# The decay tables of a retention and two-MLP kernel: loaded whole, or made on the chip from a few rows

## The chip, the core and the metric

The kernel runs on one core of one Trainium2 chip. The metric is device microseconds of one launch; the kernel before took 865.12 us, the median of three runs (864.43 to 865.42). The engines are named as in the profile: PE is TensorE, DVE is VectorE, ACT is ScalarE, POOL is GpSimd, SP is the engine that issues most loads. SPq and ACTq are the streams that issue DMAs; PEld is PE's weight load.

## What is computed

A retention layer (attention without softmax, with a decay in its place) is followed by two MLPs on the same 2304 tokens:

```
scores = scale * q @ k.T                      # 4 batches, 8 heads, 576 positions, head width 64
Dmat   = where(rel >= 0, gamma_h ** rel, 0)   # rel = position of query - position of key
x  = (scores * Dmat) @ v                      # as 2304 x 512
h  = x @ w_in;  y = max(0.01 * h, h) @ w_out  # 512 -> 2048 -> 512
h2 = y @ w2_in; out = where(h2 > 0, h2, exp(min(h2, 0)) - 1) @ w2_out
```

## The kernel before

**Tiling.** The 576 positions are cut into four chunks of 128 (`CH`) and a tail of 64, and each chunk is worked on for the four batches in turn: step `s` is chunk `s // 4`, batch `s % 4`. For a step of the first chunk (s = 0 to 3) `att_a(s)` makes the scores of 8 heads with 8 f32 products of 64x128 by 128 columns, and DVE multiplies them by the table `first` (gamma to the power of the distance, masked, times scale), into two tiles `pm`; `att_x(s)` multiplies with v; ACT rounds the sum to `xh` and DVE makes the rest `xl`. Later chunks use a running state `st`: their scores are multiplied by the table `later_sb` (line 222 and 226), and their result by the table `ot_sb` (line 281). `att_kv` updates the state; `att_w` on POOL multiplies the keys or values by decays from `sm_sb`.

**The MLPs.** Weights are loaded as 128 rows at a time and split into two parts of reduced precision: `split_a` (two ACT operations, `u` and `last`), `split_b` (four DVE operations, lines 356 to 363), `split_c` (ACT `wih` or `woh`, then `wil` or `wol` on POOL for the first four weights of each kind). `moe_h` and `moe_y` are the products of a unit of work; `moe_y` runs three units (`LAG`) behind `moe_h`, so the first three units have no `moe_y`.

**Order.** Nothing is reordered: each engine runs its instructions as they are written. The part that the change touches is the start, lines 596 to 656. Loads are issued by SP in the order written. Eight semaphores are dealt out to the loads of all queues in turn, and a load waits until the one that had its semaphore before has landed; so at most eight are in flight. `wake(n)` issues n bf16 products of 512 columns whose result nobody reads. The start is: nine wakes, `att_a(0)`, nine wakes, the split of the first weight, `att_a(1)`, `att_x(0)`, and so on to `att_kv(0)`; then come the units n = 0, 1, 2, ..., each with one `moe_h` and, while there are any, one attention step.

**Buffers.** The tag "pm" has four buffers: two for each `pm` pair and the `kn` tiles. The tag "raw" has three: `first` has one, the raw weights the others. The PSUM tags "y" and "h" have four banks each.

Of the kernel before, what the change touches and what calls it, by code (L numbers as in the profile page):

```python
# [9 lines left out]
F32 = mybir.dt.float32  # L10
# [3 lines left out]
AF = mybir.ActivationFunctionType  # L14
ALU = mybir.AluOpType

B, H, S, D = 4, 8, 576, 64
NT, DM, DFF = B * S, H * D, 2048
P = 128
NPAIR = H // 2  # L20
CH = 128
HC = CH // 2
# [17 lines left out]
WARM = 9  # L40
# [5 lines left out]
def _turned(x):  # L46

    x = x.copy()
    x[:, ::2] = np.roll(x[:, ::2], HC, axis=0)
    return x  # L50


def _decays():

    gamma = (1.0 - 2.0 ** (-5.0 - np.arange(H, dtype=np.float32))).astype(np.float64)
    scale = 1.0 / np.sqrt(D)
    pos = np.arange(CH)
    mask = (pos[None, :] >= pos[:, None]).astype(np.float64)
    ot = scale * gamma[:, None] ** (pos + 1.0 - CH)
    ot = np.repeat(ot.reshape(NPAIR, 2, 1, CH), D, axis=2)  # L60
    ot = ot.transpose(1, 2, 0, 3).reshape(P, NPAIR, CH)
    vt = _turned((gamma[:, None] ** (CH - 1.0 - pos)).T[:, :, None])[:, :, 0]
    gt = np.repeat((gamma**CH).reshape(NPAIR, 2, 1), D, axis=2).transpose(1, 2, 0).reshape(P, NPAIR)
    small = np.concatenate([vt, gt], axis=1)
    rel = pos[None, :] - pos[:, None]
    first = scale * gamma[None, :, None] ** np.maximum(rel, 0)[:, None, :] * mask[:, None, :]
    first = _turned(first).reshape(CH, NPAIR, 2, CH).transpose(2, 0, 1, 3)
    later = gamma[None, :, None] ** (CH - 1.0 - pos)[:, None, None] * mask[:, None, :]
    later = _turned(later).reshape(CH, NPAIR, 2, CH).transpose(2, 0, 1, 3)

    near = np.concatenate([later[1, :HC], later[0, HC:]]).reshape(CH, -1)
    far = np.concatenate([later[0, :HC], later[1, HC:]])[:, :, HC:].reshape(CH, -1)
    first = first.transpose(1, 0, 2, 3).reshape(CH, -1)
    later = np.concatenate([near, far], axis=1)
    return (
        np.ascontiguousarray(first, dtype=np.float32),
        np.ascontiguousarray(later, dtype=np.float32),
        np.ascontiguousarray(ot, dtype=np.float32),
        np.ascontiguousarray(small, dtype=np.float32),
    )  # L80


@with_exitstack
def retention_moe(
# [6 lines left out]
    w1_out: bass.AP,  # L91
    w2_in: bass.AP,
    w2_out: bass.AP,
    first: bass.AP,
    later: bass.AP,
    otab: bass.AP,
    small: bass.AP,
    out: bass.AP,
):
    nc = tc.nc  # L100
    NMAX = max(SIZES)
# [7 lines left out]
    gpool = ctx.enter_context(tc.tile_pool(name="gpool", bufs=2))  # L109
# [3 lines left out]
    def bank(tag, bufs):  # L113
        return psum.tile([P, 512], F32, tag=tag, bufs=bufs, name=f"ps_{tag}")
# [10 lines left out]

    pf = [cpool.tile([P, NPAIR, HC], F32, name=f"pf{j}") for j in range(2)]
    half = [slice(0, D), slice(D, P)]

# [52 lines left out]
    pm = {}  # L181
# [413 lines left out]

    with tc.manual_schedule():
        qk, v, k = slice(0, 2), slice(2, 3), slice(3, 4)
        load_step(0, [qk])
        nc.scalar.dma_start(out=sm_sb, in_=small)
        nc.sync.dma_start(out=first_sb, in_=first.rearrange("p (j n) -> p j n", j=2))  # L600
        load_next()
        load_step(1, [qk])
        load_step(0, [v])
        load_step(2, [qk])
        load_step(1, [v])
        load_step(3, [qk])
        load_step(2, [v])
        load_step(3, [v])
        load_step(0, [k])
        load_next()  # L610
        load_step(1, [k])
        load_step(4, [0])
        load_step(2, [k])
        load_step(3, [k])
        nc.sync.dma_start(out=later_sb, in_=later)
        load_step(4, [1])
        load_near(4)
        load_step(4, [2])
        nc.sync.dma_start(out=ot_sb, in_=otab)
        for z in pf:  # L620
            nc.vector.memset(z, 0.0)
        idle = pf[0].bitcast(BF16).rearrange("p a n -> p (a n)")
        warm = bank("h", 4)

        def wake(n):
            for _ in range(n):
                nc.tensor.matmul(warm, idle[:, :P], idle, start=True, stop=True)  # L627

        def step0(s):
            out_of = att_x(s, "h", 4)  # L630
            att_w(s)
            return out_of

        wake(WARM)
        att_a(0, "y", 4)
        wake(WARM)
        key = splits.pop(0)
        split_a(key)
        split_b(key)
        att_a(1, "y", 4)  # L640
        step0(0)()
        split_c(key)
        att_a(2, "y", 4)
        step0(1)()
        att_a(3, "y", 4)
        step0(2)()
        step0(3)()
        into_state = att_kv(0, "y", 4)
        del ain[0]
        load_step(5)  # L650
        load_near(5)
        load_next()
        load_near(6)
        load_near(7)
        load_next()
        begun = [splits.pop(0)]
        split_a(begun[0])
        ld, nxt = B + 2, B

        def ends_block(n):  # L660

            p = units[n - LAG] if 0 <= n - LAG < len(units) else None
            return p is not None and p[3][-1] == FQ - 1 and p[:2] != (0, 0)

        def begin(n):
            if not ends_block(n + 1) and may_split(n):
                begun.append(splits.pop(0))
                split_a(begun[-1])

        for n in range(len(units) + LAG):  # L670
            u = units[n] if n < len(units) else None
            p = units[n - LAG] if n >= LAG else None
            s = nxt if nxt < nsteps else None
            rounded, begun = begun, []
            for key in rounded:
                split_b(key)
                load_next()
            if n > 0:
                begin(n)
            else:  # L680
                att_q(nxt)
                att_w(nxt)
            if u:
                moe_h(u)
            for key in rounded:
                split_c(key)
            if n == 0:
                into_state()
                att_a(nxt, "h", 4)
                for a in range(1, B):  # L690
# [78 lines left out]
```

## Time and profile before

| | before |
|---|---|
| median of 3 runs | 865.12 us (864.43 to 865.42) |
| the profiled execution | 864.54 us, of which its span is 862.6 us |
| PE busy | 851.8 us, 99% |
| DVE busy | 503.6 us, 58% |
| ACT busy | 346.8 us, 40% |
| POOL busy | 84.3 us, 10% |
| read from HBM | 54.66 MB |
| loads of tables | `first` 512 KB, `later_sb` 384 KB, `ot_sb` 256 KB, `sm_sb` 6 KB |

All times of the trace are microseconds from the start of the span. The profiled execution took 1.9 us more than its span, and is 0.58 us below the median of the three runs. Busy shares are means over the whole span; the stages of the first 52 us differ from the rest, and have to be read by themselves.

### The profile page before, as it was taken

The page shows a single profiled execution, that of the slowest core. Times are in us where ns is not written, and L with a number is a line of the kernel's source. Part 1 is how long each engine was busy: PE and PEld are TensorE (multiplying, and loading weights), DVE is VectorE, ACT ScalarE, POOL GpSimd, SP SyncE. Part 2 cuts the span into 40 slices and gives each one's busy share as a digit, 9 for nine tenths or more (in the row PEclk, how much of TensorE's full clock was granted, in tenths as well). Part 3 has the DMA queues.
Part 4 walks back from the last instruction along what each step waited for, and adds up shares of the span by engine and source line. Part 5 has one row for each costly group of instructions (what it writes and reads, how often), then busy time and mean ns, then how long its engine had stood idle before and what let it go on. Part 6 is the DMA issues. An engine that isn't in the chain of part 4 may idle for free.

```text
span 862.6 us, 11726 instructions
## 1 busy us (share of the span) xinstructions
PE 851.8 (99%) x4664; PEld 703.6 (82%) x4664; DVE 503.6 (58%) x889; ACT 346.8 (40%) x631; POOL 84.3 (10%) x88
## 2 busy tenths in 40 slices
PE   9899999999999999999999999999999999999998
PEld 6778887888888888888888888888888888888886
DVE  5998952465254652556345863657656784675443
ACT  3445344543133432345344543554234442432222
POOL 2464421000000000002222100000000000000000
PEclk9999999999999999999999999999999999999999
DMA  9983420121000220111100220102101220001112
GB/s 337 339 289 129 172 77 11 49 98 49 1 26 23 74 74 1 49 49 65 34 24 26 74 74 0 50 29 70 49 7 43 74 74 0 25 1 49 49 50 74
DMA packets 23143, 60.15 MB, mean 70 GB/s; under 512 B 2864, under 2 KB 6192, under 8 KB 23088
## 3 DMA queue, kind: packets, MB, share of 16 engines
q1 hardware_dynamic: 22800, 59.26, 20.0%
q8 instruction: 37, 0.61, 0.3%
q10 hardware_dynamic: 288, 0.14, 0.1%
q14 instruction: 18, 0.15, 0.1%
HBM read 54.66 MB, written 4.72 MB: 69 GB/s over the span
## 4 chain that ended last, share of the span: by engine, by line
PE 96%; DVE 2%; DMA 1%; POOL 0%; ACT 0%; issue 0%; DVEq 0%
PE ps_y L537 41%; PE ps_h L398 40%; PE ps_y L477 5%; PE ps_h L425 3%; PE ps_h L430 2%; PE ps_h L204 2%; PE ps_h L250 1%; PE ps_y L204 1%; DMA ain<-in_att 1%; PE ps_h L239 0%; DVE ain L222 0%; PE ps_h L297 0%; PE ps_h L262 0%; DVE pf L226 0%; PE ps_h L627 0%; DVE raw L356 0%
## 5 line engine op out<-in xcount | busy, mean ns | idle before, releaser
L398 PE MATMUL ps_h<-xh,wil 128*128 128x512 f32 x512 | 199.6, 390 | 1.1 <-POOL wil L374 1.1
L398 PE MATMUL ps_h<-xh,wih 128*128 128x512 f32 x512 | 199.9, 390 | 0.7 <-ACT wih L372 0.5
L412 DVE TENSOR_TENSOR gl<-g,gh 128x512 fp32r<-128x512 f32 x128 | 91.0, 711 | 173.2 <-ACT g L406 167.6
L398 PE MATMUL ps_h<-xl,wih 128*128 128x512 f32 x512 | 136.9, 389 | 0.0
L410 DVE SCALAR_TENSOR_TENSOR g<-g,ps_h 128x512 f32<-128x512 f32 x64 | 44.0, 687 | 122.1 <-ACT g L409 121.9
L405 ACT ACTIVATE gh<-ps_h 128x512 fp32r<-128x512 f32 x64 | 38.2, 597 | 188.8 <-PE ps_h L398 188.8
L398 PEld LDWEIGHTS ps_h<-xh,wil 128*128 128x128 f32 x512 | 96.1, 188 | 21.5 <-POOL wil L374 1.8
L398 PEld LDWEIGHTS ps_h<-xh,wih 128*128 128x128 f32 x512 | 96.1, 188 | 21.3 <-ACT wih L372 0.7
L398 PEld LDWEIGHTS ps_h<-xl,wih 128*128 128x128 f32 x512 | 96.1, 188 | 20.2
L408 ACT ACTIVATE g<-ps_h 128x512 f32<-128x512 f32 x64 | 38.2, 597 | 180.1 <-PE ps_h L398 180.0
L537 PE MATMUL ps_y<-gh,woh 128*128 128x512 f32 x256 | 101.3, 396 | 0.5 <-ACT woh L372 0.5
L537 PE MATMUL ps_y<-gh,wol 128*128 128x512 f32 x256 | 100.1, 391 | 0.6 <-POOL wol L374 0.6
L537 PE MATMUL ps_y<-gl,woh 128*128 128x512 f32 x256 | 99.8, 390 | 0.0
L537 PE MATMUL ps_y<-woh,gl 128*128 128x512 f32 x256 | 99.7, 390 | 0.0
L537 PE MATMUL ps_y<-wol,gh 128*128 128x512 f32 x256 | 99.7, 390 | 0.0
L537 PE MATMUL ps_y<-woh,gh 128*128 128x512 f32 x256 | 99.6, 389 | 0.0
L552 DVE TENSOR_TENSOR yp<-yp,ps_y 128x512 f32<-128x512 f32 x96 | 59.4, 681 | 0.0
L537 PEld LDWEIGHTS ps_y<-gh,wol 128*128 128x128 f32 x256 | 48.0, 188 | 11.4 <-POOL wol L374 1.1
L537 PEld LDWEIGHTS ps_y<-gh,woh 128*128 128x128 f32 x256 | 48.0, 188 | 11.3 <-ACT woh L372 0.7
L537 PEld LDWEIGHTS ps_y<-woh,gl 128*128 128x128 f32 x256 | 48.1, 188 | 10.0
L537 PEld LDWEIGHTS ps_y<-wol,gh 128*128 128x128 f32 x256 | 48.1, 188 | 9.9
L537 PEld LDWEIGHTS ps_y<-woh,gh 128*128 128x128 f32 x256 | 48.0, 188 | 9.8
(106 smaller groups left out, 1104.2 us busy)
## 6 DMA issues: line engine op xcount, KB each, us to landing
raw<-in_moe_in SPq DMA_DIRECT2D x32, 512.0 KB, 3.3
raw<-in_moe_out SPq DMA_DIRECT2D x32, 512.0 KB, 3.3
ain<-in_att SPq DMA_DIRECT2D x16, 512.0 KB, 6.4
ain<-in_att SPq DMA_DIRECT2D x20, 256.0 KB, 7.2
out<-yp SPq DMA_DIRECT2D x17, 256.0 KB, 2.2
kn<-in_att SPq DMA_DIRECT2D x12, 256.0 KB, 6.3
st<-in_near_v SPq DMA_DIRECT2D x32, 64.0 KB, 5.0
ain<-in_tail_qk SPq DMA_DIRECT2D x4, 256.0 KB, 3.4
```

What stands on the lines that cost most here:

```text
L204: nc.tensor.matmul(sc[j][keys[j], pr * n : (pr + 1) * n], t[r, 1, pr * n : (pr + 1) * n], t[r, 0, pr * n : (pr + 1) * n], start=True, stop ...
L250: nc.tensor.matmul(x[half[j], pr * n : (pr + 1) * n], st[b][:, j, pr, :], t[:, 2 * j, pr * n : (pr + 1) * n], start=pr == 0, stop=n < CH, ...
L398: nc.tensor.matmul(h[:, i * n : (i + 1) * n], a, x, start=k == 0, stop=k == len(ops) - 1)
L405: nc.scalar.activation(gh, h, AF.Prelu, alpha=0.01)
L408: nc.scalar.activation(g, h, AF.Relu, scale=-1.0)
L410: nc.vector.scalar_tensor_tensor(g, g, -1.0, h, ALU.add, ALU.max)
L412: nc.vector.tensor_tensor(gl, g, gh.bitcast(F32), ALU.subtract)
L425: nc.tensor.matmul(h, wh[:, w], xx[:, kk, :], start=kk == 0, stop=False, skip_group_check=True)
L430: nc.tensor.matmul(h[:, :n], wl[:, w], xh[blk][:, kk, :], start=False, stop=kk == KC - 1, skip_group_check=True,)
L477: nc.tensor.matmul(o, a, x, start=f == 0 and k == 0, stop=f == FQ - 1 and k == len(ops) - 1, skip_group_check=True,)
L537: nc.tensor.matmul(y[e], a, x, start=f == 0 and k == 0, stop=f == FQ - 1 and k == 2)
L552: nc.vector.tensor_tensor(t, t, y[e], ALU.add)
```

## The change

The three tables `first`, `later_sb` and `ot_sb` are no longer loaded. The host gives instead 8 rows of `keys` (8 x 256), 8 rows of `queries` (8 x 1024), 2 rows of `otab` (2 x 512), and `small`, which now also holds a mask of 128 x 256. On the chip:

- `load_tables` issues six loads from ACT's queue, where one stood, and ahead of all others in the program.
- `table_first`: for each of two halves one f32 product of an 8x128 weight by 512 columns on PE, and a DVE multiplication with the mask into `first_sb`. It stands after the nine wakes and before `att_a(0)`.
- `table_later`: four POOL multiplications of 64 rows (512, 256, 512, 256 columns) of mask by decay into `later_sb`.
- `table_out`: one f32 product of a 2x128 weight by 512 columns on PE and an ACT copy into `ot_sb`. It stands after `att_a(0)`. The second group of wakes has four products where it had nine.
- The rows lie in buffers that are used later: `rows_k` (keys and mask) and `rows_o` in two "pm" buffers, `rows_q` in the two of the tag "g".

```diff
@@ -119,3 +119,48 @@
+    rows_k = apool.tile([P, NPAIR, CH], F32, tag="pm", name="rows_k", bufs=4)
...
+    rows_o = apool.tile([P, NPAIR, CH], F32, tag="pm", name="rows_o", bufs=4)
...
+    rows_q = [gpool.tile([P, NMAX], F32, tag="g", name="rows_q") for _ in range(2)]
+
+    def load_tables():
+        nc.scalar.dma_start(out=rows_k[:H, : 2 * P], in_=keys)
+        for j in range(2):
+            nc.scalar.dma_start(
+                out=rows_q[j][:H, :], in_=queries[:, j * NPAIR * CH : (j + 1) * NPAIR * CH]
+            )
+        nc.scalar.dma_start(out=rows_k[:, 2 * P :], in_=small[:, H + NPAIR :])
+        nc.scalar.dma_start(out=sm_sb, in_=small[:, : H + NPAIR])
+        nc.scalar.dma_start(out=rows_o[:2, :], in_=otab)
+
+    def table_first():
+        for j in range(2):
+            t = bank("y", 4)
+            nc.tensor.matmul(t, rows_k[:H, :P], rows_q[j][:H, :], start=True, stop=True)
+            nc.vector.tensor_tensor(
+                first_sb[:, j, :].rearrange("p (a n) -> p a n", a=NPAIR),
+                t.rearrange("p (a n) -> p a n", a=NPAIR),
+                mask[:, j, :].unsqueeze(1).to_broadcast([P, NPAIR, CH]),
+                ALU.mult,
+            )
+
+    def table_out():
+        t = bank("h", 4)
+        nc.tensor.matmul(t, rows_k[:2, P : 2 * P], rows_o[:2, :], start=True, stop=True)
+        nc.scalar.activation(ot_sb, t.rearrange("p (a n) -> p a n", a=NPAIR), AF.Copy)
+
+    def table_later():
+        v = decay_v.rearrange("p (a j) -> p j a", j=2)
+        for j in range(2):
+            for r, to, cut in ((half[1 - j], near_w, slice(0, CH)), (half[j], far_w, slice(HC, CH))):
+                n = cut.stop - cut.start
+                nc.gpsimd.tensor_tensor(
...
@@ -595,9 +634,8 @@
+        load_tables()
         load_step(0, [qk])
-        nc.scalar.dma_start(out=sm_sb, in_=small)
-        nc.sync.dma_start(out=first_sb, in_=first.rearrange("p (j n) -> p j n", j=2))
         load_next()
...
-        nc.sync.dma_start(out=later_sb, in_=later)
...
-        nc.sync.dma_start(out=ot_sb, in_=otab)
...
         wake(WARM)
+        table_first()
+        table_later()
         att_a(0, "y", 4)
-        wake(WARM)
+        table_out()
+        wake(WARM // 2)
         key = splits.pop(0)
```

DVE, from its first product of scores to the second step's. In the kernel before (`pm` are the masked scores of steps 0 and 1, `raw`, `u` and `last` the split of the first weight):

```order
L216 TENSOR_TENSOR pm_156<-ps_y_146,first_100 128x512 [waits DMAHW2_49,PE_49]
L216 TENSOR_TENSOR pm_157<-ps_y_147,first_100 128x512 [waits PE_49]
L356 TENSOR_SCALAR raw_107<-raw_107 128x512 [waits DMAHW3_49,Activation_49]
L358 TENSOR_SCALAR u_169<-u_169 128x512
L361 SCALAR_TENSOR_TENSOR u_169<-u_169,raw_107 128x512 [waits DVE_49]
L363 ISA u_169<-u_169,last_171 128x1024 [waits DVE_49,Activation_49]
L216 TENSOR_TENSOR pm_187<-ps_y_177,first_100 128x512 [waits PE_49]
```

And now, with the line numbers of the changed kernel (216 is 255 there, 356 to 363 are 395 to 402):

```order
L144 TENSOR_TENSOR first_104<-ps_y_152,rows_k_91 128x512 [waits DMAHW5_49,PE_49]
L144 TENSOR_TENSOR first_104<-ps_y_155,rows_k_91 128x512 [waits PE_49]
L255 TENSOR_TENSOR pm_172<-ps_y_162,first_104 128x512 [waits DVE_49,PE_49]
L255 TENSOR_TENSOR pm_173<-ps_y_163,first_104 128x512 [waits DMAHW7_49,DVE_49,PE_49]
L395 TENSOR_SCALAR raw_115<-raw_115 128x512 [waits DMAHW4_49,Activation_49]
L397 TENSOR_SCALAR u_183<-u_183 128x512
L400 SCALAR_TENSOR_TENSOR u_183<-u_183,raw_115 128x512 [waits DVE_49]
L402 ISA u_183<-u_183,last_185 128x1024 [waits DVE_49,Activation_49]
L255 TENSOR_TENSOR pm_201<-ps_y_191,first_104 128x512 [waits DMAHW0_49,PE_49,Pool_49]
```

Two multiplications stand ahead of the first `pm`. `pm_173` is given the buffer of `rows_o`, so it waits for that load (DMAHW7) and for the PE product of `table_out` that reads it; `pm_201` is given the buffer of `rows_k`, so it waits for the POOL passes that read the mask there.

ACT, from its first instruction to the first rounding `xh`. In the kernel before:

```order
L599 DMA sm_sb_83<-in_small 128x12
L344 ACT_TABLE_LOAD
L344 ACTIVATE u_169<-raw_107 128x512 [waits DMAHW3_49]
L346 ACTIVATE last_171<-raw_107 128x512
L275 ACTIVATE xh0_91<-ps_h_191 128x4x128 [waits PE_49]
```

And now (344 and 346 are 383 and 385 there):

```order
L131 DMA rows_k_91<-in_keys 8x256
L133 DMA rows_q_93<-in_queries 8x512
L133 DMA rows_q_94<-in_queries 8x512
L136 DMA rows_k_91<-in_small 128x256
L137 DMA sm_sb_83<-in_small 128x12
L138 DMA rows_o_92<-in_otab 2x512
L154 ACT_TABLE_LOAD
L154 ACTIVATE ot_sb_82<-ps_h_176 128x512 [waits PE_49]
L383 ACTIVATE u_183<-raw_115 128x512 [waits DMAHW4_49]
L385 ACTIVATE last_185<-raw_115 128x512
```

The copy of `ot_sb`, which waits for PE, now stands ahead of the split of the first weight. On SP the loads of steps 0 to 3 keep their order, but the third load of all, the queries and keys of step 1, now has a wait in front of it, where the first seven had none:

```order
L186 DMA ain_113<-in_att 128x1024
L375 DMA raw_115<-in_moe_in 128x1024
L186 DMA ain_117<-in_att 128x1024 [waits DMAHW0_49]
L186 DMA ain_113<-in_att 128x512 [waits DMAHW1_49]
L186 DMA ain_120<-in_att 128x1024 [waits DMAHW2_49]
```

DMAHW0 is the semaphore of the load of `keys`, DMAHW1 that of step 0's own queries and keys, DMAHW2 that of the first half of `queries`.

## Rows read from the trace of the kernel before

**Rows 1.** The page: span, engines (busy, share, instructions), chain of waits by engine.

```profile
span 862.6 us, 11726 instructions
PE 851.8 (99%) x4664; PEld 703.6 (82%) x4664; DVE 503.6 (58%) x889; ACT 346.8 (40%) x631; POOL 84.3 (10%) x88
...
PE 96%; DVE 2%; DMA 1%; POOL 0%; ACT 0%; issue 0%; DVEq 0%
```

**Rows 2.** Stages: length; PE, PEld, DVE, ACT, POOL busy; clock; DMA share, GB/s.

```profile
9.29:18.19 8.90, 8.27 (x129) 7.01 (x128) 7.27 (x12) 2.96 (x6) 4.97 (x5) 1.00 1.04 400
...
36.89:52.28 15.39, 12.89 (x154) 10.18 (x154) 14.81 (x25) 8.19 (x14) 9.45 (x11) 1.00 1.03 349
52.28:862.60 810.32, 806.66 (x4132) 669.57 (x4132) 462.46 (x816) 323.95 (x593) 62.05 (x62) 1.00 0.16 52
```

**Rows 3.** DVE's waits, all of them, from 9.3 to 52.28: total, times, longest.

```profile
DVE gl L412 <- ACT g L406: 1.3, 1, 1.3
DVE xl L276 <- ACT xh L275: 1.1, 1, 1.1
DVE pm L216 <- PE ps_h L239: 0.3, 2, 0.2
```

**Rows 4.** Timeline of DVE: start, length, instruction, [idle before it <- releaser].

```profile
7.28 1.29 DVE L216 TENSOR_TENSOR pm<-ps_y,first 128x512 f32<-128x512 f32 x2 [5.87 <-PE ps_y L204]
8.48 0.42 DVE L356 TENSOR_SCALAR raw<-raw 128x512 uint32<-128x512 uint32 x1
...
10.71 1.41 DVE L216 TENSOR_TENSOR pm<-ps_y,first 128x512 f32<-128x512 f32 x2
```

**Rows 5.** Timeline of PE, the start and the end of the first stages.

```profile
1.19 4.02 PE L627 MATMUL ps_h<-pf 128*128 128x512 bf16 x9 [1.19 <-DVE pf L621]
5.27 1.97 PE L204 MATMUL ps_y<-ain 64*128 64x128 f32 x16
7.18 2.12 PE L627 MATMUL ps_h<-pf 128*128 128x512 bf16 x9
9.22 1.16 PE L204 MATMUL ps_y<-ain 64*128 64x128 f32 x16
...
35.01 1.16 PE L204 MATMUL ps_h<-ain 64*128 64x128 f32 x16 [1.20 <-DMA ain<-in_att]
...
36.89 0.50 PE L398 MATMUL ps_h<-xh,wil 128*128 128x512 f32 x1 [0.28 <-POOL wil L374]
...
52.28 0.50 PE L537 MATMUL ps_y<-gh,wol 128*128 128x512 f32 x1 [0.62 <-POOL wol L374]
```

**Rows 6.** Timeline of ACT: its DMA issue, and the split of the first weight.

```profile
0.73 0.40 ACTq L599 DMA_DIRECT2D sm_sb<-in_small  x1
...
7.74 0.67 ACT L344 ACTIVATE u<-raw 128x512 f32<-128x512 f32 x1 [5.29 <-DMA raw<-in_moe_in]
8.32 0.67 ACT L346 ACTIVATE last<-raw 128x512 uint32<-128x512 uint32 x1
11.48 0.60 ACT L275 ACTIVATE xh<-ps_h 128x512 fp32r<-128x512 f32 x1 [2.50 <-PE ps_h L239]
```

**Rows 7.** DMA issues: tile, queue, times, KB each, us from issue to landing.

```profile
first<-in_first SPq DMA_DIRECT2D x1, 512.0 KB, 5.3
...
out<-yp ACTq DMA_DIRECT2D x1, 128.0 KB, 1.7
sm_sb<-in_small ACTq DMA_DIRECT2D x1, 6.0 KB, 4.7
```

**Rows 8.** Timeline of POOL, three shapes.

```profile
11.53 1.04 POOL L188 TENSOR_TENSOR ain<-ain,sm_sb 128x512 f32<-128x512 f32 x1 [11.09 <-PE ps_h L239]
...
29.14 1.29 POOL L315 TENSOR_TENSOR st<-st,sm_sb 64x256 f32<-64x256 f32 x2
...
39.16 1.28 POOL L283 TENSOR_TENSOR xl<-xt,xh 128x512 fp32r<-128x512 f32 x1
```

**Rows 9.** Timeline of DVE while POOL's pass at 39.16 runs.

```profile
39.30 1.42 DVE L356 TENSOR_SCALAR raw<-raw 128x512 uint32<-128x512 uint32 x1
```

More of the change, by code (lines that the diff above doesn't have):

```diff
@@ L57, in _decays @@
     pos = np.arange(CH)
[L58 to L62, printed above, removed]
-    gt = np.repeat((gamma**CH).reshape(NPAIR, 2, 1), D, axis=2).transpose(1, 2, 0).reshape(P, NPAIR)
[L64 to L80, printed above, removed]
+    ot = (scale * gamma[:, None] ** (pos + 1.0 - CH)).reshape(NPAIR, 2, CH).transpose(1, 0, 2)
+    gt = np.repeat((gamma**CH).reshape(NPAIR, 2, 1), D, axis=2).transpose(1, 2, 0).reshape(P, NPAIR)
+    key = np.where(np.arange(H) % 2 == 0, np.roll(pos, HC)[:, None], pos[:, None])
+    vt = gamma ** (CH - 1.0 - key)
+    mask = (pos[None, None, :] >= key[:, :2, None]).reshape(CH, -1)
+    small = np.concatenate([vt, gt, mask], axis=1)
+    keys = np.concatenate([gamma[:, None] ** -(key.T * 1.0), np.zeros((H, P))], axis=1)
+    keys[0, P : P + D] = 1.0
+    keys[1, P + D :] = 1.0
+    queries = np.zeros((H, 2, NPAIR, CH))
+    for h in range(H):
+        queries[h, h % 2, h // 2] = scale * gamma[h] ** (1.0 * pos)
+    tables = small, keys, queries.reshape(H, -1), ot.reshape(2, -1)
+    return tuple(np.ascontiguousarray(a, dtype=np.float32) for a in tables)
 @with_exitstack
@@ L93, in retention_moe @@
     w2_out: bass.AP,
-    first: bass.AP,
-    later: bass.AP,
+    small: bass.AP,
+    keys: bass.AP,
+    queries: bass.AP,
     otab: bass.AP,
-    small: bass.AP,
     out: bass.AP,
@@ L127, in retention_moe @@
     half = [slice(0, D), slice(D, P)]
+    rows_k = apool.tile([P, NPAIR, CH], F32, tag="pm", name="rows_k", bufs=4)
+    rows_k = rows_k.rearrange("p a n -> p (a n)")
+    mask = rows_k[:, 2 * P :].rearrange("p (j n) -> p j n", j=2)
+    rows_o = apool.tile([P, NPAIR, CH], F32, tag="pm", name="rows_o", bufs=4)
+    rows_o = rows_o.rearrange("p a n -> p (a n)")
+    rows_q = [gpool.tile([P, NMAX], F32, tag="g", name="rows_q") for _ in range(2)]
[28 more added lines that the diff above has]
+                nc.gpsimd.tensor_tensor(
+                    to[r],
+                    mask[r, j, cut].unsqueeze(1).to_broadcast([D, NPAIR, n]),
+                    v[r, j, :].unsqueeze(2).to_broadcast([D, NPAIR, n]),
+                    ALU.mult,
+                )
     ain, kn = {}, {}
@@ L737 @@
     near = near.reshape(B, NMAIN, HC, NPAIR, 2, D).transpose(0, 1, 4, 2, 3, 5)[:, :, ::-1]
-    first, later, otab, small = _decays()
+    small, keys, queries, otab = _decays()
     arrays = {
@@ L742 @@
         "near_v": near.reshape(B, NMAIN, P, NPAIR * D),
-        "first": first,
-        "later": later,
+        "small": small,
+        "keys": keys,
+        "queries": queries,
         "otab": otab,
-        "small": small,
     }
@@ L760 @@
     order = ["att", "tail_qk", "near_v", "moe_in", "moe_out", "moe2_in", "moe2_out"]
-    order += ["first", "later", "otab", "small"]
+    order += ["small", "keys", "queries", "otab"]
     with tile.TileContext(nc) as tc:
```

## The prediction

> **What bounds the kernel now.** I read the page first, then a table of stages, then the timelines of the start. By the page PE is busy 99% of the span and carries 96% of the chain of waits [rows 1]. So work that is taken off the DMA queues gains nothing in general; it gains only where PE waits. The table of stages says where that is: from 52.28 us to the end PE is busy 806.7 of 810.3 us, while the loads use 16% of the DMA engines [rows 2]. Those 810 us come out the same whatever the change does; the question is when they begin. At 52.28 PE waits for the last time, for the second part of a weight, `wol` [rows 5]. That weight comes off DVE's split (then ACT, then POOL), and from 36.89 to 52.28 DVE is busy 14.8 of 15.4 us [rows 2]. Ahead of it, DVE's waits from 9.3 to 52.28 come to 2.7 us in all, for ACT and PE, and none is for a load [rows 3]. So although the DMA engines are full in these stages (share about 1.0, 350 to 400 GB/s), the chain that sets the start of the long PE stretch is DVE's: it runs from the first `pm` at 7.28 [rows 4] through the splits and masks of the first units. What delays DVE early delays everything.
>
> **What is removed.** 1,152 KB of tables are not loaded, and about 176 KB of rows and mask are (8 x 256, 8 x 1024, 2 x 512, 128 x 268 floats), against 6 KB before: 0.98 MB net, some 2.5 us of DMA at 400 GB/s [rows 2]. As DVE waits for no load, I cost this gain at nothing; the cover is DVE's own work. The one wait of PE for a load of a later step, 1.20 us at 35.01, is followed at 36.89 by a wait for `wil` from the DVE chain [rows 5], so it gives nothing either. Five wakes fewer take 1.2 us off PE (2.12/9 each), but not off the chain, as DVE will be the later one.
>
> **The new products on PE.** Each is an f32 product of 512 columns with few rows. No row shows one. The nearest is `att_a`: 8 f32 products of 128 columns, in two halves of the array's rows, in 1.16 us at 9.22, and in 1.97 us at 5.27 [rows 5]. If the halves run one after the other, 512 columns cost half of that, 0.55; if side by side, all of it, 1.1 us. I take 0.94, four times a wake's 0.236, near the upper end, because the halves sit on different rows, and slightly below it, because short products pay their start eight times. Early on, PE is slower: the same wake takes 0.447 us in the first group (4.02/9) and 0.236 in the second [rows 5], the levels of 1.2 and 2.4 GHz, though the clock column reads 1.00 throughout; `att_a(0)`, which followed 4 us of wakes, still ran at the lower level to about 7.2. At that level I take 4 x 0.447 = 1.79 us.
>
> The Trainium skill, page "FP8 and Floating Point Precision", section "TensorE Precision Notes", says that a true fp32 product makes four passes through the array. By it a product would cost the 0.94 taken here; the trace has two records for each f32 product, and by two passes it would cost 0.47, which is the first rival below.
>
> **The start, step by step.** The wakes end at 5.21 as before. The first table product then needs `keys` and half of `queries`, issued by ACT at 0.73 and about 1.15 (0.40 an issue [rows 6]). The nearest landings are 1.7 us (128 KB at a quiet time) and 4.7 us (6 KB in this very place) [rows 7], so 2.9 to 5.9 us; most of that lies under the wakes, and I take 5.25.
> - First table product 5.25 to 7.04 (1.79, low level). Second: 0.16 us at the low level, the rest at the high one, to 8.06. `att_a(0)` 1.16, to 9.2. The product of `table_out` 0.94, to 10.15.
> - DVE: two new multiplications by the mask, 0.69 each as L216, at 7.1 and 8.1: they lie in DVE's wait for PE. The mask, issued fourth at about 2.0, lands by 7.3 if it takes the 5.3 us of `first` [rows 7]; no harm is done before 8. The first `pm` runs 9.25 to 9.95. The second waits for the product of `table_out`, whose buffer it takes: 10.2 to 10.9.
> - ACT: the copy of `ot_sb` waits for the same product, and the split of the first weight is queued behind it, though its data are there by then: copy 10.2 to 10.8 (0.60 as L275), `u` starts some 0.55 later than the copy, as rows of ACT follow each other, and ends at 11.4 (0.67) [rows 6].
> - DVE's first split operation waits for `u`: 11.4 where it was 8.48 [rows 4], **2.9 us late**. All that follows on DVE (rest of the split, `pm` of steps 1 to 3, `xl`) waits behind it.
>
> Given back: DVE's two waits of 0.16 us for PE, 0.3 [rows 3], since PE is now ahead. Loads of steps 1 to 3 wait in SP's queue for landings of tables, the first to about 5.4; they are needed 2 to 3 us later than before and there is less ahead of them, so I cost that at nothing (if the cover were gone, each us of late landing past 10.9 for step 1 would be a us). So the last `pm`, the first `moe_h`, and everything up to 52.28 come 2.9 - 0.3 = **2.6 us later**.
>
> **POOL.** The four passes of `table_later` start when mask and `sm_sb` have landed, at about 7.3, and cost two of 64x512 and two of 64x256. By L188 and L315 that is 2 x 1.04 + 1.29 = 3.4 us [rows 8], by the 1.28 of L283 3.9: they end at 10.7 to 11.2, before `att_w(0)`, before the buffer of the mask is wanted by the third `pm` (13.6), and just before the split's L356 at 11.4. If they are later, L356 can be held up: at 39.30 it took 1.42 us instead of 0.42, while a POOL pass ran from 39.16 to 40.44 [rows 4, 8, 9]. I take 0, and up to 1.0 for the range.
>
> The Trainium skill, page "SBUF — State Buffer", section "Who interferes with whom", says that a `tensor_scalar` in its fast mode and a GpSimd operation exclude each other for a whole instruction. That is what the 1.42 shows, and it speaks against moving passes to POOL in this place; by it alone the sum would be up to 3.6 us.
>
> **Sum.** The profiled execution took 864.54 us (862.6 of it span), which is 0.58 below the median. 864.54 + 2.6 = 867.1 for a profiled run; on the median 865.12 + 2.6 = **867.7 us**.
>
> **Rivals.**
> - *The products are cheap.* 0.47 us (0.89 at the low level): products to 6.14 and 7.03, `att_a(0)` to 8.2, `table_out` to 8.7, copy and `u` to 9.95, the split 1.5 late, less 0.3: +1.2, **866.3 us**. For it: two records per product, 0.55 as one bound. Against: halves on different rows. A clock that rises earlier than in this run does much the same.
> - *The clock rises later.* In this run it rose at about 7.2 us, after the wakes and `att_a(0)` [rows 5]; from 5.25 on other products now stand there. If PE is at 1.2 GHz until the second wakes: products to 7.04 and 8.83, `att_a(0)` 1.97 to 10.8, `table_out` 1.79 to 12.6, `u` to 13.9: 5.4 late, less 0.3: +5.1, **870.2 us**. For it: two of the products ahead of the rise are of a kind that no row shows. Against: PE is as busy from 1.19 to 7.2 as it was.
> - *The loads decide (faster).* PE's loads and the DMA engines are full to 52.28; if the arrival of weights and steps sets DVE's pace behind what the releasers show, 0.98 MB less gives back its 2.5 us: **862.6 us**. It decides if the start's 2.9 us of delay are hidden by loads that come that much later than their users, that is, if DVE in the kernel before had waits for loads. For it: DMA share 1.0. Against: not one such wait after 9.3 [rows 3].
>
> **Chances.** Forecast 0.60, cheap products 0.21, later clock 0.11, loads 0.08. The range goes from 865.7 (below the cheap products by half their shift) to 870.3 (the later clock): it leaves out the loads, some of the cheap products and what lies above. About 0.2%, 1.7 us, is what a measurement of this kernel can tell from no change: 863.4 to 866.85 is "same". That takes nearly all of the cheap products and 0.08 to 0.09 of the forecast (a shift under 1.7), 0.29; faster 0.08; slower 0.63.
>
> **What would show it.** DVE's first split operation at 11 to 12 us instead of 8.48, with an idle stretch ahead of it that ACT's `u` ends; ACT's `u` right behind the copy of `ot_sb`; the second `pm` behind the product of `table_out`; the two table products at 1.8 and 1.0 us; the last wait for `wol` at about 54.9 instead of 52.28, and the same 810 us behind it. Wrong it would be if the first `moe_h` starts no later than before (18.2 us), if PE or DVE after 12 us wait for loads, or if POOL's passes end after 12 us and hold L395.

## The result, and the profile after

The changed kernel took 870.12 us, the median of four runs (868.91 to 871.32), and the kernel before beside it 865.07 us (864.43 to 865.42): a ratio of 1.0057, 95% interval 1.0045 to 1.0069, or 5.05 us more. The forecast was 867.7, in a range of 865.7 to 870.3: the sign was right and the time lies inside, but the shift is twice the 2.6 us forecast. The four runs form two groups, 869.06 and 868.91, 871.17 and 871.32: the median lies between them, where no run does, and the upper group lies above the range. The profile here is that of the run of 869.06 us; the other group has one below.

The page of the changed kernel (answers to [rows 1]): the span is 4.6 us longer, and the chain is as much PE's as before.

```profile
span 867.2 us, 11739 instructions
...
PE 96%; DVE 1%; DMA 1%; POOL 1%; ACT 0%; issue 0%; SPq 0%; ACTq 0%; DVEq 0%
```

The timeline of PE (start, length, line, form, [idle before it <- releaser]); L143 are the two table products of `first`, L153 that of `table_out`, L663 the wakes, L243 `att_a`, L278 `att_x`, L437 `moe_h`, L576 `moe_y`:

```profile
5.43 2.12 PE L143 MATMUL ps_y<-rows_q,rows_k 8*128 8x512 f32 x4 [0.60 <-DMA rows_q<-in_queries]
7.47 1.90 PE L243 MATMUL ps_y<-ain 64*128 64x128 f32 x16
9.30 2.07 PE L153 MATMUL ps_h<-rows_o,rows_k 2*128 2x512 f32 x2
11.30 1.89 PE L663 MATMUL ps_h<-pf 128*128 128x512 bf16 x4
13.12 1.82 PE L243 MATMUL ps_y<-ain 64*128 64x128 f32 x16
...
22.75 0.49 PE L437 MATMUL ps_h<-xh,wih 128*128 128x512 f32 x1 [0.22 <-ACT xh L314]
...
56.87 0.50 PE L576 MATMUL ps_y<-gh,wol 128*128 128x512 f32 x1 [0.63 <-POOL wol L413]
```

The first `moe_h` starts at 22.75 instead of 18.19, 4.56 us later; the last wait for `wol` ends at 56.87 instead of 52.28 [rows 5], 4.59 later. Behind it the same 810.3 us follow as in [rows 2], by the table of stages (columns as there):

```profile
56.87:867.20 810.33, 806.67 (x4132) 669.57 (x4132) 462.54 (x816) 324.30 (x593) 62.13 (x62) 1.00 0.16 52
```

So all of the loss arises ahead of the first `moe_h`. The timeline also shows how: four wakes take 1.89 us, 0.47 each, twice the 0.236 of the second group in [rows 5], and both `att_a` take 1.8 to 1.9 instead of 1.16. The table of stretches for PE says when (stretch, length, PE busy, granted clock, DMA share, GB/s):

```profile
5.50:7.50 2.00, 2.00 (x6) 1.00 1.05 372
7.50:8.00 0.50, 0.50 (x7) 0.71 0.99 369
...
8.50:14.00 5.50, 5.50 (x24) 0.50 0.98 329
...
14.50:15.00 0.50, 0.50 (x10) 0.96 1.07 438
```

The granted clock was 1.00 while the table products ran, and they took 1.06 us each. It fell to 0.50, the level of 1.2 GHz, at about 7.7 us, and stayed there to 14.5, although PE was busy in all of that time. Before the fall PE had run the products of 8 rows and begun `att_a(0)`; the product of 2 rows, four wakes and `att_a(1)` followed in the low stretch. In the profile of the kernel before, the clock, once up at about 7.2 us, does not fall again.

In this profile the clock falls once more, at about 41.8, for 3.4 us, among products of 128 rows and behind waits of PE of 0.64 and 0.86 us:

```profile
42.00:42.50 0.50, 0.50 (x2) 0.50 1.08 270
```

It costs next to nothing there, as the last wait for `wol` is late by no more than the first `moe_h` was. But it shows that products of few rows are not all that a fall can stand behind. a_rows128 below has the same two waits (0.64 and 0.86 us) and no such fall; what brings this one about was not examined.

DVE, ACT and POOL (answers to [rows 4], [rows 6] and [rows 8]); L395 is the first split operation, L255 `pm`, L154 the copy of `ot_sb`, L383 `u`, L161 the four passes:

```profile
9.40 0.69 DVE L255 TENSOR_TENSOR pm<-ps_y,first 128x512 f32<-128x512 f32 x1 [1.12 <-PE ps_y L243]
11.41 0.69 DVE L255 TENSOR_TENSOR pm<-ps_y,first 128x512 f32<-128x512 f32 x1 [1.32 <-PE ps_h L153]
12.58 0.43 DVE L395 TENSOR_SCALAR raw<-raw 128x512 uint32<-128x512 uint32 x1 [0.48 <-DMA ain<-in_att]
```

```profile
11.41 0.60 ACT L154 ACTIVATE ot_sb<-ps_h 128x512 f32<-128x512 f32 x1 [6.90 <-PE ps_h L153]
11.90 0.65 ACT L383 ACTIVATE u<-raw 128x512 f32<-128x512 f32 x1
```

```profile
7.76 3.38 POOL L161 TENSOR_TENSOR later_sb<-rows_k,sm_sb 64x512 f32<-64x512 f32 x4 [7.32 <-DMA sm_sb<-in_small]
```

The order is as forecast: the second `pm` and ACT's copy wait for the product of `table_out` at the same moment (11.41), `u` stands right behind the copy, and DVE's split waits for `u`, which ends at 12.55 (the row names a DMA as the one that came last; in a_again the same wait is put down to ACT's `u`). It starts at 12.58, where the forecast had 11.4 and the kernel before 8.48. POOL's passes end at 11.14 and hold nothing up.

### The profile page after: what moved, and what is told of

It is laid out like the page before. It is cut to its first block, busy times and chain, and to the rows that moved or that the text cites. A ratio compares the mean times of both kernels' runs of the same rounds, so it can differ in the third digit from the quotient of the medians.

```text
span 867.2 us, 11739 instructions
## 1 busy us (share of the span) xinstructions
PE 857.2 (99%) x4665; PEld 705.9 (81%) x4665; DVE 506.0 (58%) x891; ACT 347.7 (40%) x632; POOL 87.6 (10%) x92
## 4 chain that ended last, share of the span: by engine, by line
PE 96%; DVE 1%; DMA 1%; POOL 1%; ACT 0%; issue 0%; SPq 0%; ACTq 0%; DVEq 0%
PE ps_y L576 41%; PE ps_h L437 40%; PE ps_y L516 5%; PE ps_h L464 3%; PE ps_h L469 2%; PE ps_h L243 1%; PE ps_h L289 1%; PE ps_y L243 1%; PE ps_h L278 0%; DMA ain<-in_att 0%; DMA rows_q<-in_queries 0%; PE ps_h L336 0%; PE ps_h L301 0%; DVE ain L261 0%; POOL wil L413 0%; PE ps_y L143 0%
## 5 line engine op out<-in xcount | busy, mean ns | idle before, releaser
L437 PE MATMUL ps_h<-xh,wih 128*128 128x512 f32 x512 | 200.5, 392 | 0.9 <-ACT wih L411 0.6
L437 PE MATMUL ps_h<-xh,wil 128*128 128x512 f32 x512 | 200.3, 391 | 0.9 <-POOL wil L413 0.9
L437 PE MATMUL ps_h<-xl,wih 128*128 128x512 f32 x512 | 137.4, 390 | 0.0
L437 PEld LDWEIGHTS ps_h<-xh,wih 128*128 128x128 f32 x512 | 96.4, 188 | 21.5 <-ACT wih L411 0.8
L437 PEld LDWEIGHTS ps_h<-xh,wil 128*128 128x128 f32 x512 | 96.5, 188 | 21.1 <-POOL wil L413 1.3
L437 PEld LDWEIGHTS ps_h<-xl,wih 128*128 128x128 f32 x512 | 96.6, 189 | 20.4
L576 PE MATMUL ps_y<-gh,woh 128*128 128x512 f32 x256 | 101.3, 396 | 0.5 <-ACT woh L411 0.5
L576 PE MATMUL ps_y<-gh,wol 128*128 128x512 f32 x256 | 100.1, 391 | 0.6 <-POOL wol L413 0.6
L576 PE MATMUL ps_y<-gl,woh 128*128 128x512 f32 x256 | 99.8, 390 | 0.0
L576 PE MATMUL ps_y<-woh,gl 128*128 128x512 f32 x256 | 99.7, 390 | 0.0
L576 PE MATMUL ps_y<-wol,gh 128*128 128x512 f32 x256 | 99.7, 390 | 0.0
L576 PE MATMUL ps_y<-woh,gh 128*128 128x512 f32 x256 | 99.6, 389 | 0.0
L576 PEld LDWEIGHTS ps_y<-gh,wol 128*128 128x128 f32 x256 | 48.0, 188 | 11.3 <-POOL wol L413 1.1
L576 PEld LDWEIGHTS ps_y<-gh,woh 128*128 128x128 f32 x256 | 48.0, 188 | 11.3 <-ACT woh L411 0.7
L576 PEld LDWEIGHTS ps_y<-woh,gl 128*128 128x128 f32 x256 | 48.1, 188 | 10.0
L576 PEld LDWEIGHTS ps_y<-woh,gh 128*128 128x128 f32 x256 | 48.0, 188 | 9.8
L576 PEld LDWEIGHTS ps_y<-wol,gh 128*128 128x128 f32 x256 | 48.0, 188 | 9.8
```

The lines of the kernel that those rows point to most:

```text
L437: nc.tensor.matmul(h[:, i * n : (i + 1) * n], a, x, start=k == 0, stop=k == len(ops) - 1)
L576: nc.tensor.matmul(y[e], a, x, start=f == 0 and k == 0, stop=f == FQ - 1 and k == 2)
```

## Experiments

Theories. **A, the clock:** the order costs what was forecast; the rest is PE at 1.2 GHz after products of few rows. **B, the order alone:** the delay is `table_first` and `table_out` standing ahead of the split, whatever the clock does. **C, the loads:** the tables' rows push the loads of the steps and weights back. The kernel before took 864.8 us beside all of these. All kernels compute the whole result.

### The changed kernel again (no edit): a_again, a_look1, a_look2

> The changed kernel once more, unaltered, as the measure for the next three. Times of 868.9 to 871.3 us are expected, in two groups 2.2 us apart as before (869.0 and 871.2). Both theories below hold that what differs between the groups is TensorE's granted clock in the first 15 us; if the profiled run is one of the slow group, its granted clock should be 0.5 from the table products at 5.4 us on (products 2.1 us each, not 1.06), and the first product of the experts should start at some 24 us and not at 22.75.

> The changed kernel, unaltered, for a profile of its slower group (870.8 to 871.3 us; two in five runs so far). If this one falls in it, Theory A expects from a_rows128b, whose profiled run was 2 us longer than its other runs: PE pauses for over 1 us ahead of the table products and they then take 1.8 to 2.1 us each, while the clock column reads 1.00. If it falls in the faster group: as a_again, 868.9 us.

> The changed kernel, unaltered, once more, for the same purpose: 868.9 us with the first product of the experts at 22.6 to 22.8, or 870.8 to 871.3 with it at some 24.7 us and table products of 1.8 to 2.1 us each.

Measured: a_again 868.85, 868.84, 870.79, 870.86, 868.88; a_look1 870.31; a_look2 871.04. The profile of a_again is like the one above, with the clock low from about 8.4 to 15.2 and the first `moe_h` at 22.62. a_look2 shows the slower group. Its timeline of PE:

```profile
5.23 3.75 PE L143 MATMUL ps_y<-rows_q,rows_k 8*128 8x512 f32 x4
8.91 2.08 PE L243 MATMUL ps_y<-ain 64*128 64x128 f32 x16
10.92 2.07 PE L153 MATMUL ps_h<-rows_o,rows_k 2*128 2x512 f32 x2
12.92 1.89 PE L663 MATMUL ps_h<-pf 128*128 128x512 bf16 x4
14.73 2.08 PE L243 MATMUL ps_y<-ain 64*128 64x128 f32 x16
...
24.93 0.50 PE L437 MATMUL ps_h<-xh,wih 128*128 128x512 f32 x1 [0.22 <-ACT xh L314]
```

Here the clock did not rise before about 17 us: wakes of 0.47 us still at 12.92, table products of 1.87. (The clock column reads 1.00 for these stretches, as it does for the first wakes of every profile; the durations tell the level.) DVE's split starts at 14.20. The products did not wait for their rows this time, so the pause that the expectation named is not what makes this group. In a_look1 the clock was up for the table products and then low from about 7.4 to 17.6: first `moe_h` at 24.20. So one kernel has three courses of the clock in the start, and the first `moe_h` at 22.7, 24.2 and 24.9; the spans follow (867.1, 868.5, 869.3).

### The table products over 128 rows: a_rows128, a_rows128b

```diff
+        (memsets of rows_q, rows_k[:, :2P] and rows_o to zero, ahead of the loads;
+         a_rows128b: behind those of the wakes' operands, and more of them on POOL)
-            nc.tensor.matmul(t, rows_k[:H, :P], rows_q[j][:H, :], start=True, stop=True)
+            nc.tensor.matmul(t, rows_k[:, :P], rows_q[j], start=True, stop=True)
-        nc.tensor.matmul(t, rows_k[:2, P : 2 * P], rows_o[:2, :], start=True, stop=True)
+        nc.tensor.matmul(t, rows_k[:, P : 2 * P], rows_o, start=True, stop=True)
```

> The changed kernel, with the three table products made over all 128 rows (the rows below the 8 and the 2 are set to zero first); the output is the same. Theory A (the clock: after the products of 8 and 2 rows PE is granted 1.2 GHz from 7.7 to 14.5 us): the clock stays at 1.00, products 5.4 to 7.5, att_a(0) 1.16 to 8.7, the product of table_out 1.03 to 9.7, ACT's copy and u to 10.9, DVE's split at 10.9 where it was 12.58; time 867.2 to 868.0 us. Theory B (the order alone: whatever the rows, the split stands behind table_out, and the clock falls because PE paused for 0.60 us ahead of the products, or in any case): clock and times as in the changed kernel, split at 12.6, 869 to 871 us. Theory C (loads: the tables' loads push those of the steps back): as B, 869 to 871 us.

> The changed kernel with the three table products over all 128 rows, as a_rows128, but with the zeros written so that they don't hold up the start: the two memsets ahead of the wakes stay first on DVE, and GpSimd writes most of the zeros. In a_rows128 the wakes began at 2.27 us instead of 1.19 and the table products at 6.56 instead of 5.21 to 5.43. Theory A (the clock falls after products of 8 and 2 rows, and zeros in the other rows are enough to keep it up): clock 1.00 to the end of the start, products from 5.4 to 5.8 us on, DVE's split at 10.9 to 11.2, the first product of the experts at 20.1 to 20.4 (22.75 in the changed kernel, 18.19 before); 866.7 to 867.4 us. Theory B (the lower clock is not what costs the second half): 868 to 869 us although the clock stays up.

Measured: a_rows128 867.83 us (867.36 to 869.72), ratio 1.0041 [1.0027, 1.0054]; a_rows128b 867.48 (867.24 to 869.36), 1.0035 [1.0022, 1.0049]. From a_rows128, PE, DVE's split and the stretches of PE:

```profile
6.56 1.96 PE L143 MATMUL ps_y<-rows_q,rows_k 128*128 128x512 f32 x4 [0.27 <-DMA rows_q<-in_queries]
8.44 1.16 PE L243 MATMUL ps_y<-ain 64*128 64x128 f32 x16
9.53 1.12 PE L153 MATMUL ps_h<-rows_o,rows_k 128*128 128x512 f32 x2
...
21.21 0.50 PE L437 MATMUL ps_h<-xh,wih 128*128 128x512 f32 x1 [0.22 <-ACT xh L314]
```

```profile
11.88 0.43 DVE L395 TENSOR_SCALAR raw<-raw 128x512 uint32<-128x512 uint32 x1 [0.49 <-ACT u L383]
```

```profile
6.50:8.40 1.90, 1.84 (x4) 1.00 1.01 323
8.40:12.50 4.10, 4.10 (x39) 1.00 0.94 269
```

The same instructions in the same order, with zeros in the other rows: the clock stays up, `att_a` is back at 1.16, `table_out` at 1.12. The memsets hold up the wakes, so the table products start 1.13 us later than in the profile above (6.56 for 5.43), and yet DVE's split starts at 11.88 instead of 12.58 and the first `moe_h` at 21.21 instead of 22.75. An estimate: without those 1.13 us it would be at 20.1, 1.9 us behind the kernel before. B and C, which expected no change, fall for this part of the loss. The expectation gave B a second reason for the fall, the pause of 0.60 us ahead of the table products. Two of the kernels below speak against it: in a_rows128_late PE pauses 0.59 us in that place, in a_first_loaded 0.76 ahead of `att_a(0)` and 0.91 ahead of `att_a(1)`, and in both the clock stays up through the start.

a_rows128b was to remove the delay, but its profiled run (869.36 us, one of its two longer ones) had PE wait 1.33 us for the rows of `queries`, and the clock low to begin with:

```profile
6.54 3.75 PE L143 MATMUL ps_y<-rows_q,rows_k 128*128 128x512 f32 x4 [1.33 <-DMA rows_q<-in_queries]
10.22 1.25 PE L243 MATMUL ps_y<-ain 64*128 64x128 f32 x16
```

That is the counterpart of a_look2: both enter the table products at 1.2 GHz (3.75 us for two); behind 128 rows the clock is up in `att_a(0)` (1.25), behind 8 rows it is not (2.08), and was not for 8 us more. a_wake9 below is nearer still: 8 rows, a pause of 1.03 us, and 2.08. The three faster runs of a_rows128b, 867.24 to 867.48, lie just under the forecast of 867.7, whose sum had the clock up; but none of them was profiled, and they are still 2.5 us above the kernel before. So no run shows the products over 128 rows without a late start, and the 1.9 us stay an estimate.

### Few rows in the kernel before: b_low_wakes

```diff
-        wake(WARM)                       # the second group of nine
+        wake(WARM, H)                    # the same, with idle[:8] as operands
```

> The kernel before; only the second group of nine wakes (7.18 to 9.3 us) feeds 8 rows of the array instead of 128. The result of the wakes is never read, so what is computed is the same; order, loads and number of instructions too, and the products are bf16. Theory A (few rows bring the clock down): the granted clock falls to 0.50 some time after 8 us and comes back by 14, att_a(1) takes 2.0 instead of 1.16 and the first product of the experts starts 0.5 to 2 us later than at 18.19; 865.3 to 867 us. Theory B (it is the f32 table products, or the order, that bring it down): clock 1.00 to 22 us, 864.3 to 865.4 us as before.

Measured: 866.99 us (864.55 to 868.09), ratio 1.0020 [1.0012, 1.0029], so 2.2 us more than the kernel before. PE and its stretches:

```profile
6.67 2.11 PE L627 MATMUL ps_h<-pf 8*128 8x512 bf16 x9
9.11 1.87 PE L204 MATMUL ps_y<-ain 64*128 64x128 f32 x16 [0.33 <-DMA ain<-in_att]
10.91 1.97 PE L239 MATMUL ps_h<-pm,ain 128*64 128x128 f32 x16
```

```profile
6.60:9.00 2.40, 2.18 (x13) 1.00 1.02 411
9.00:9.50 0.50, 0.39 (x6) 0.88 1.07 434
9.50:12.50 3.00, 3.00 (x30) 0.50 1.03 402
12.50:13.00 0.50, 0.50 (x6) 0.71 1.04 385
```

The eight-row wakes themselves take what those of 128 rows take (2.11), but the clock falls at about 9.4 and stays low to 12.8; the first `moe_h` starts at 19.66, 1.47 late. Nothing else was changed: not the kind of the products, the order or the loads. So eight rows in place of 128 brought the clock down; A holds here too. (PE paused 0.33 us just ahead of the fall; the 0.91 us of a_first_loaded, behind wakes of 128 rows in the same place, brought none.) It need not happen in every run: of eleven, ten took 865.85 to 868.09, and one, not profiled, 864.55, as the kernel before.

### `table_out` later, and both edits: a_out_late, a_rows128_late

```diff
         att_a(0, "y", 4)
-        table_out()
         wake(WARM // 2)
...
                     att_kv(a, "y", 4)()
                     del ain[a]
+                table_out()
     (rows_o and a copy of two rows of keys lie in buffers that are free by then)
```

> The changed kernel, with table_out moved from the start to behind the att_kv of step 3, where step 4 first needs it (its rows and its weights lie in buffers that are free by then); the output is the same. Theory A (the clock and the order each carry part): the clock still falls after the two products of 8 rows, so att_a(0) ends at 9.4, the two pm at 10.8, the split starts at 10.8 (12.58 in the changed kernel, 8.48 before) and pm of step 1 at 13.1: 867.3 to 868.2 us. Theory B (the order alone, the wait for table_out being all of the delay): the split starts behind pm of step 0 at no more than 9.5, 865.5 to 866.5 us. Theory C (loads): unchanged, 869 to 871 us.

> Both edits of the two kernels above together: table_first over 128 rows, and table_out behind the att_kv of step 3; the output is the same. Theory A: the clock stays at 1.00, att_a(0) ends at 8.7, the pm at 9.4 and 10.1, the split starts at 10.1, 1.6 us later than in the kernel before; 866.3 to 867.0 us, what is left being the two products of table_first, 2.1 us of PE ahead of att_a(0), less 0.5 that the higher clock gives back. Theory B: as table_out late alone, 865.5 to 866.5. Theory C (loads): unchanged, 869 to 871 us.

Measured: a_out_late 866.38 us (865.76 to 868.71), ratio 1.0020 [1.0012, 1.0029]; a_rows128_late 867.65 (867.17 to 867.94), 1.0033 [1.0020, 1.0046]. The first lies in the band of B, but not for B's reason alone: its clock fell later than A assumed, behind `att_a(0)`, and for a shorter time.

```profile
5.50:9.00 3.50, 3.49 (x22) 0.99 1.03 346
9.00:12.00 3.00, 3.00 (x19) 0.50 0.98 291
```

So moving `table_out` takes away both its own place ahead of the split and most of the low stretch, and this run can't share the 2.5 us out between the two. The second kernel was expected at 866.3 to 867.0, and came out no better than a_rows128b. DVE's timeline, and POOL's, say why:

```profile
10.74 0.75 DVE L396 TENSOR_SCALAR raw<-raw 128x512 uint32<-128x512 uint32 x1
11.42 0.84 DVE L398 TENSOR_SCALAR u<-u 128x512 f32<-128x512 f32 x1
...
13.12 1.31 DVE L403 CUSTOM_DVE_ANT_0 u<-u,last 128x1024 uint16<-128x1024 uint16 x1
```

```profile
8.50 3.47 POOL L162 TENSOR_TENSOR later_sb<-rows_k,sm_sb 64x512 f32<-64x512 f32 x4 [7.45 <-DMA sm_sb<-in_small]
12.77 1.12 POOL L228 TENSOR_TENSOR ain<-ain,sm_sb 128x512 f32<-128x512 f32 x1 [0.80 <-POOL later_sb L162]
```

The split now starts at 10.74, 1.14 us earlier than in a_rows128, but beside POOL's passes: its first two operations take 0.75 and 0.84 us where in the kernel before both take 0.42 [rows 4 has the first], and its last, beside POOL's next operation, 1.31 instead of 0.69. That is 1.4 us, more than the earlier start had brought. By the rule of the Trainium skill that the prediction weighed (page "SBUF — State Buffer", section "Who interferes with whom"), a `tensor_scalar` in its fast mode and a GpSimd operation exclude each other. The first two operations, 0.75 and 0.84 us, agree with it.

### One part alone: a_only_first, a_first_loaded

a_only_first makes `first` on the chip and loads the other two tables; a_first_loaded loads `first` and makes the others:

```diff
a_only_first:    - table_later() - table_out(), - wake(WARM // 2) + wake(WARM), + loads of later_sb and ot_sb
a_first_loaded:  - table_first(), table_out() behind att_kv of step 3, wake(WARM), + load of first_sb,
                 load_tables() behind load_step(0)
```

> Only `first` is made on the chip, by the two products of 8 rows and the mask; `later` and `ot` are loaded as in the kernel before, and all nine wakes are kept. Theory A: products 5.4 to 7.5, att_a(0) to 8.7, the split at 9.9 to 10.1 (1.5 late); the clock still falls after 8 us, but the nine wakes of 128 rows follow; 866.0 to 867.0 us, about as a_out_late (866.38), so that the passes on GpSimd cost nothing. Theory B (GpSimd's passes, or table_out, cost what a_out_late still loses): 864.5 to 865.5 us.

> The part of the changed kernel that saves loads without products ahead of att_a(0): `first` is loaded as in the kernel before (0.5 MB), `later` made by GpSimd's four passes, `ot` by one product of 2 rows behind the att_kv of step 3, all nine wakes; 0.6 MB less is loaded than before. Theory A (PE's products in the start are the whole cost, and fewer loads bring nothing): the split starts at 8.5 to 9.0, held up a little by GpSimd's passes, and the first product of the experts at 18.2 to 18.8; 864.5 to 865.6 us, as before within 0.1%. Theory C (loads decide): 863 us or less. If GpSimd's passes were what costs, it would be 866 or more.

Measured: a_only_first 867.51 us (866.45 to 869.73), ratio 1.0038 [1.0025, 1.0051]; a_first_loaded 866.47 (866.32 to 868.18), 1.0023 [1.0013, 1.0032].

The median of a_only_first lies above the bands of both theories. Its profiled run (866.45) is one without a fall of the clock: the nine wakes of 128 rows, at 8.73, take 2.12 us. What delays it is the mask, which DVE's table multiplication waits for: it starts at 8.59, and the split at 10.99. Its runs spread over 3.3 us, as those of a kernel with more than one course; only the fastest was profiled.

```profile
8.59 1.29 DVE L150 TENSOR_TENSOR first<-ps_y,rows_k 128x512 f32<-128x512 f32 x2 [7.18 <-DMA rows_k<-in_small]
```

a_first_loaded is a miss for A and for C, and a hit for the side remark on GpSimd. It has no product ahead of `att_a(0)` and 0.5 MB less to load, and is still 1.7 us slower than the kernel before. ACT's `u` and DVE's split:

```profile
8.50 0.67 ACT L383 ACTIVATE u<-raw 128x512 f32<-128x512 f32 x1 [4.71 <-DMA raw<-in_moe_in]
```

```profile
9.20 1.26 DVE L395 TENSOR_SCALAR raw<-raw 128x512 uint32<-128x512 uint32 x1 [0.67 <-ACT u L383]
10.38 0.84 DVE L397 TENSOR_SCALAR u<-u 128x512 f32<-128x512 f32 x1
```

The raw weight lands 0.76 us later (`u` at 8.50 for 7.74, [rows 6]), though its load is issued at 1.65 in both kernels; and POOL's passes (7.46 to 10.93) cost the split 1.26 us. Together 2.0 us at the end of the split, 1.6 at the first `moe_h` (19.79). That the mask's 128 KB, issued at 0.73 and so ahead of the first weight, make it late is likely, but was not tried alone. So the POOL part costs nothing in the changed kernel only because the split is late there for other reasons.

### One product, and the wakes: a_out128, a_wake9

```diff
a_out128:  the product of table_out over 128 rows (memsets of its operands); table_first stays at 8 rows
a_wake9:   - wake(WARM // 2)  + wake(WARM)
```

> The changed kernel; only the product of table_out runs over 128 rows (126 of them zeros), those of table_first stay at 8 rows. Theory A, first form (the product of 2 rows is what makes the clock's fall as long as it is; without it, as in a_out_late, the fall is from 9 to 12.2 us only): granted clock 0.50 over some 3 us instead of 6.5, first product of the experts at 21.0 to 21.9 instead of 22.6 to 22.75, 867.4 to 868.3 us. Second form (the products of 8 rows alone bring the fall, and its length is fixed): as the changed kernel, 868.8 to 870.9 us.

> The changed kernel with all nine wakes in the second group again, where it has four. In a_only_first, where nine wakes of 128 rows came soon after the products of 8 rows, the clock did not fall. Theory A, if the missing wakes let it fall: clock 1.00 again, the first product of the experts at 20.5 to 21.5, 867 to 868 us. If the product of 2 rows ahead of the wakes is enough: the clock falls at 8 us as in the changed kernel, and the five wakes more lie at 0.43 us each ahead of att_a(1): its pm wait up to 1.5 us longer, 869.5 to 872 us.

Measured: a_out128 869.28 us (868.06 to 870.36), ratio 1.0049 [1.0035, 1.0063]; a_wake9 871.95 (870.09 to 872.81), 1.0072 [1.0057, 1.0087]. The profiled run of a_out128 (868.06) speaks for the first form, its median for the second:

```profile
9.50:12.50 3.00, 3.00 (x6) 0.50 0.78 261
```

The fall was half as long there (9.3 to 12.6), but one profile of six runs does not show that it is so in the others: which of the two kinds of product sets its length stays open. a_wake9 falls in the second band of its expectation: nine wakes behind the product of `table_out` do not keep the clock up. It is 1.3 us slower than a_again in the faster runs of each (870.09 and 870.17 for 868.84 to 868.88). Its profile, of its longest run, shows how five more wakes at the low clock come to lie on the path: the clock was low from the first wake to about 17.5, the nine take 3.80 us, and DVE waits for the `att_a(1)` behind them.

```profile
6.24 3.75 PE L143 MATMUL ps_y<-rows_q,rows_k 8*128 8x512 f32 x4 [1.03 <-DMA rows_q<-in_queries]
9.91 2.08 PE L243 MATMUL ps_y<-ain 64*128 64x128 f32 x16
```

```profile
18.90 0.69 DVE L255 TENSOR_TENSOR pm<-ps_y,first 128x512 f32<-128x512 f32 x1 [1.38 <-PE ps_y L243]
```

No kernel here is faster than the one before.

## Why the prediction was half right

**What bounds: right.** All of the loss is there at the first `moe_h` (4.56 of 4.6 us); the 810.3 us behind the last wait are the same; DVE's first split operation stands later for the reason given, `u` behind the copy of `ot_sb` behind the product of `table_out`. Of the signs named, these came true and three were off in size: the split at 12.58 (11 to 12), the last wait for `wol` at 56.87 (54.9), the table products at 1.06 us each (1.8 and 1.0).

**The price of a product: right.** 0.94 and 1.79 us were taken from the wake; 1.06 was measured at the high level, 1.87 and 2.07 at the low one. The rival of cheap products, 0.47, is out. The Trainium skill, page "FP8 and Floating Point Precision", section "TensorE Precision Notes", gives four passes for a true fp32 product; the trace agrees, with 1.06 us against 0.94 for four wakes.

**The loads: right on waits, with one reservation.** DVE waited for none after 9.3 us but one of 0.5 us, the one just told of at 12.58. None of the eight variants that load less came out faster than the kernel before, so the rival of 862.6 is out. (The rows and the mask come to 178 KB, where the prediction has about 176; the 0.98 MB stands.) But `queries` landed anywhere from in time for 5.21 to 6.24 (a_wake9, whose loads are those of the changed kernel), where one value, 5.25, was taken. That lies on the path: from a_look2 to a_wake9, both at the low clock, the products start 1.01 us later (5.23 and 6.24), and the split 1.00 (14.20 and 15.20).

**POOL: right, but by luck of place.** Ending at 11.14 (forecast 10.7 to 11.2), the passes missed the split. Where the split ran beside them they cost it 1.26 us (a_first_loaded), above the bound of 1.0, and 0.75 (a_rows128_late, 1.4 with POOL's next operation).

**The step that failed: the clock.** The sum took it to rise at 7.2 us and to stay up. In the profiled run it was up earlier, at the table products, and then fell for 7 us. With the clock up from the table products on (a_rows128, its late start taken off) the first `moe_h` is 1.9 us late, by estimate: that is the order and the products, for which the forecast had 2.6, 0.85 of it because it put the first product at the low level (1.79 for 0.94). By the same estimate the other 2.6 or 2.7 us of the 4.56 are the low clock, which the forecast had at nothing: 0.7 in `att_a(0)` (1.90 for 1.16) and 1.0 in the product of `table_out` (2.07 for 1.06), both ahead of the split, and 0.8 behind it, where DVE waits for PE: from the split to the first `moe_h` it is 10.17 us here and 9.33 in a_rows128. (In the kernel before it is 9.71: the 0.3 that the forecast gave back came in a_rows128 and not here.) What a run shows without anything taken off is less: zeros in the rows bring the first `moe_h` forward by 1.54 us. In a_look2, 6.74 us late at the first `moe_h`, the low clock is some 4.8 of it, by the same estimate.

**The rival had it for the slower group, and the range held by it.** "The clock rises later" gave products to 7.04 and 8.83, `att_a(0)` to 10.8, `table_out` to 12.6, `u` to 13.9 and 870.2 us. a_look2 has 8.91, 10.92, 12.92, the split at 14.20, and 871.0. The prediction named what spoke for it, products of a kind that no row showed in the place where the clock rises, and set against it that PE is as busy as it was. That argument is the error: PE was busy in all of 8.5 to 14.0 us and ran at half speed. For the faster group no rival stood ready, as none had the clock fall after it had risen. And that 870.12 lies inside the range is luck: its upper end, 870.3, was drawn by this rival's 870.2, to which the chances gave 0.11, and not by the mechanism of the forecast.

**"Five wakes fewer ... not off the chain": wrong.** They are worth 1.3 us in the changed kernel (a_wake9). The reason, that at the low clock `att_a(1)` is later than DVE, is seen in the profile of its longest run (DVE waits 1.38 us there, 0.38 in a_look2 with four wakes); its faster runs have no profile.

## What to carry to other kernels

A product of a few rows cost PE what a full one costs (two of 8 rows 2.12 us, two of 128 rows 1.96), and it can cost the clock besides; where such products stand in the start, ahead of short work that everything waits for, price what follows at both levels. Zeros in the unused rows were enough to keep the clock up in each of the three profiles whose start had them in all its table products, and bought 1.4 us here (868.88 to 867.48, medians of a_again and a_rows128b). And transfers that nobody waited for gave nothing back: no kernel that loads less was faster, while each product, copy and pass put in their place met the one chain that mattered, or missed it only by where it happened to stand.

## What the runs showed of the hardware

- Behind products of 8 and 2 rows the granted clock fell to 0.50 with PE busy throughout (from 7.7 to 14.5 us). In the kernel before, with nine 8-row bf16 wakes in place of full ones, it fell from 9.4 to 12.8, after a pause of 0.33. Behind the f32 products with zeros in the other rows it did not fall in the start (a_rows128, a_rows128_late, a_rows128b, one profile each).
- Where nine wakes of 128 rows followed the 8-row products soon (a_only_first, one profile), there was no fall.
- The clock also fell among products of 128 rows, later in the run (changed kernel, from about 41.8 to 45.3 us, behind waits of PE of 0.64 and 0.86 us); a_rows128 had the same waits and no fall.
- One program had three courses of the clock in its first 17 us: up and down again (to 14.5 or 15.2), the same and longer (to 17.6), and low from the first wake to about 17. From the first to the last it is 2.2 us of the time.
- With a POOL operation running, `tensor_scalar` operations of 0.42 us took 0.57 (a_out_late) to 1.26 (a_first_loaded), and the split's last operation, on 16-bit words, 1.31 instead of 0.69.
